# Weights four rows to a partition, X kept in the same order of columns: windowed attention with sinks and a highway layer on one core

## The chip, the cores and the metric

The kernel runs on one core of a Trainium2 chip. The metric is the time of one execution in microseconds (us) of device time; shorter is better. A core has five engines that matter here. TensorE (PE) multiplies matrices; its loads of weights are a row of their own (PEld). VectorE (DVE) and ScalarE (ACT) work element by element. GpSimd (POOL) does so too, and it also issues the loads that change the type on their way. SyncE (SP) issues other transfers. Sixteen DMA engines move the data between the chip's memory and the core's. The profile comes from one execution; the times come from several.

## What is computed

There are 4 batches of 8 heads, 768 positions and a head dimension of 64. Each query sees the 128 newest keys up to its own and the first 4 keys (the sinks). The heads of a position, side by side, are the 512 features of a token; a highway layer follows over the 3072 tokens.

```python
keep = is_sink | in_window            # in_window: 0 <= i - j < 128, is_sink: j < 4
a = softmax(where(keep, q @ k.T / 8, -1e9))
x = (a @ v)                           # (4, 8, 768, 64) -> (3072, 512)
H = maximum(x @ w_h, 0)
T = 1 / (1 + exp(-(x @ w_t + b_t)))
out = T * H + (1 - T) * x
```

All inputs and the output are float32. The kernel computes in float16 with sums in float32.

## The kernel before, in words

The work is cut into 24 tiles of 128 tokens, six to a batch. A loop over the steps n (lines 593 to 691) keeps three tiles in work: in step n the scores of tile n, the value products of tile n-1 and the highway layer of tile n-2. The order of the instructions on each engine is the order in which the program writes them (line 741 fixes it), so an instruction that waits holds up everything behind it on its engine.

**On PE, in a step:** the masks (line 308) and score products of tile n (line 333), the bias of the gate (line 371), the sinks' share (line 379) and the value products of tile n-1 (lines 432 and 435), the gate of tile n-2 (line 471, weight `wt`), half of its hidden layer (line 492, weight `wh`), four transpositions of X of tile n-1 (line 461), and the other half of the hidden layer. Tiles 0 to 3 are handled apart: their gates run in steps 2 to 5, their hidden layers in steps 4 to 6 (lines 611, 659, 664), because `wh` comes late.

**On ACT:** the exponential of a tile's scores (line 421), the tanh of the gate (line 479), and the copy of the transposed X out of PSUM (line 466).

**On DVE:** the normalization (lines 443 and 445) divides the value products by their sums and writes X of the tile; `diff` (line 505) computes max(h, 0) - X into `DD`; `gated` (line 510) multiplies it by the gate; and `transpose_qk` (line 133) turns Q and K, which come in with rows of tokens, in blocks of 32 by 32.

**On POOL:** `finish` (line 516) adds X to the gated difference and gives float32; `cast_v` (line 150) turns V to float16 from step 6 on; `sink_values` (lines 290 and 291); and all issues of Q, K and weight loads that change float32 to float16 (lines 117, 204, 208). These issues go round eight semaphores in turn, and each waits until the load eight places earlier has landed. The output goes out from SP.

X is a tile of 128 tokens by 512 features in their natural order. The weights lie with feature kc * 128 + p in partition p, part kc, and the transposition of X takes 128 neighbouring columns at a time, so that both sides of the products meet. The program's preamble (lines 180 to 208) issues the first loads in the order: Q and K of the first segment of batch 0, K of the second, `wt`, the bias row, Q and K of the third, `wh`. The first loads of batch 1 come in step 2 (lines 623 to 625), further ones by a table (lines 559 to 561), and the places of the transpositions by another (lines 547 to 556) and by the lines 636 to 651.

Of the kernel before, what the change touches and what calls it, by code (L numbers as in the profile page):

```python
# [10 lines left out]
FP16 = mybir.dt.float16  # L11
# [3 lines left out]
ALU = mybir.AluOpType  # L15
# [22 lines left out]
def kernel(  # L38
# [13 lines left out]
    P = 128  # L52
    pe, act, dve, pool, sp = nc.tensor, nc.scalar, nc.vector, nc.gpsimd, nc.sync

    B, H, S, D = q.shape
# [5 lines left out]
    NT, DM = out.shape  # L61
# [57 lines left out]
            in_=(q, k)[which][b, :, t0:t0 + nt, :].rearrange(  # L119
                "(hg g) (r m) d -> g r hg (m d)", g=G, m=nt // 32)[g])  # L120

    def load_rows(b, i, which):
        for g in range(G):
            load_part(b, i, g, which)

    def transpose_qk(b, i, which, hgs=slice(0, HG)):
# [22 lines left out]
    def cast_v(n, engine):  # L149
        engine.tensor_copy(out=v_of(n)[:, :, 0:D], in_=V32[n])  # L150
# [50 lines left out]
    load_sinks(0, range(2, G))  # L201
    make_identity(nc, ident)
    load_rows(0, 1, 1)
    pool.dma_start(out=wt, in_=moe_w_t.rearrange("(kc p) of -> p kc of", p=P))
    pool.dma_start(out=brow[0:P:32, :], in_=moe_b_t.unsqueeze(0).to_broadcast([G, DM]))
    load_rows(0, 2, 0)
    load_rows(0, 2, 1)
    pool.dma_start(out=wh, in_=moe_w_h.rearrange("(kc p) of -> p kc of", p=P))

    dve.memset(ebias, _EXP_BIAS)  # L210
    for g in range(1, G):
# [68 lines left out]
    def sink_keys(b, engine=pool):  # L280
        for hg in range(HG):
            engine.tensor_tensor(
                out=sk[:, b, hg, :, 1],
                in0=tr[b][:, 1, hg, 0:NSINK, :].rearrange("p s e -> p e s").unsqueeze(2)
                .to_broadcast([P, 2, G, NSINK]),
                in1=skmask.unsqueeze(1).unsqueeze(3)
                .to_broadcast([P, 2, G, NSINK]), op=ALU.mult)

    def sink_values(b):
        pool.tensor_copy(out=vs32[64:P, b, 0:D], in_=vs32[0:64, b, 0:D])  # L290
        pool.tensor_tensor(
            out=vs[b], in0=vs32[:, b].unsqueeze(1).to_broadcast([P, H, D + 1]),
            in1=vmask.unsqueeze(2).to_broadcast([P, H, D + 1]), op=ALU.mult)
# [146 lines left out]
    def norm(n):  # L440
        rec = work.tile([P, HG, G], FP32, tag="rec", name="rec")
        av = sums(n)[:, :, 0:G * (D + 1)].rearrange("p hg (g e) -> p hg g e", e=D + 1)
        dve.reciprocal(out=rec, in_=av[:, :, :, D])
        X[n] = work.tile([P, HG, G, D], FP16, tag="X", name="X", bufs=10)
        dve.tensor_tensor(out=X[n], in0=av[:, :, :, 0:D],  # L445
                          in1=rec.unsqueeze(3).to_broadcast([P, HG, G, D]), op=ALU.mult)

    XT = [None] * N

# [6 lines left out]

    def x_transpose(n):
        xt = turned(n)
        x = X[n].rearrange("p hg g d -> p (hg g d)")
        for kc in range(KC):  # L460
            pe.transpose(xt[:, kc // 2, (kc % 2) * P:(kc % 2 + 1) * P],  # L461
                         x[:, kc * P:(kc + 1) * P], ident)

    def x_copy(n):
        XT[n] = work.tile([P, KC * P], FP16, tag="XT", name="XT")
# [30 lines left out]

    O = [None] * N

    def flat(x, cols):
        return x.rearrange("p hg g d -> p (hg g d)")[:, cols]  # L500

    def diff(n, cols=slice(0, DM), h=None):
        if DD[n] is None:
            DD[n] = work.tile([P, DM], FP16, tag="DD", name="DD", bufs=8)
        dve.scalar_tensor_tensor(out=DD[n][:, cols], in0=ps_h[:, cols] if h is None else h,  # L505
                                 scalar=0.0, in1=flat(X[n], cols),
                                 op0=ALU.max, op1=ALU.subtract)

    def gated(n, cols=slice(0, DM)):
# [3 lines left out]
    def finish(n, cols=slice(0, DM), eng=pool, queue=sp):  # L513
        if O[n] is None:
            O[n] = work.tile([P, DM], FP32, tag="O", name="O")
        eng.tensor_tensor(out=O[n][:, cols], in0=DD[n][:, cols], in1=flat(X[n], cols),  # L516
                          op=ALU.add)
        queue.dma_start(out=out[n * P:(n + 1) * P, cols], in_=O[n][:, cols])

# [9 lines left out]
    def finish_twice(n, cols=slice(0, DM), queue=sp):  # L529
        if O[n] is None:  # L530
            O[n] = work.tile([P, DM], FP32, tag="O", name="O")
        dve.scalar_tensor_tensor(out=O[n][:, cols], in0=DD[n][:, cols], scalar=0.5,  # L532
                                 in1=flat(X[n], cols), op0=ALU.mult, op1=ALU.add)
        queue.dma_start(out=out[n * P:(n + 1) * P, cols], in_=O[n][:, cols])

    def complete(m):
# [20 lines left out]
    issues = [(b, i, g, which) for b in range(1, B) for i in range(len(segments[b]))  # L557
              for which in range(2) for g in range(G)][2 * G:]
    loads = {}
    for n, count in zip(range(2, 17), [4] * 4 + [3] * 7 + [2] + [3] * 3):  # L560
        loads[n] = [issues.pop(0) for _ in range(count)]
    assert not issues
    v_at = {1: (2,), 2: (3,), 3: (4,), 4: (5,), 5: (6, 7), 6: (8, 9)}
# [23 lines left out]
    transpose_qk(0, 1, 0)  # L587
    cast_v(0, dve)
    sink_keys(0, dve)

    idle(18)
    last = N - 1
    for n in range(last):

        nb, n1 = n - 2, n - 1
        joined = n < 5 or n >= 7
        before = (n1 if 0 <= n1 < N else None, nb if nb >= 0 else None)
        if n < N:
            after = opening(n, *before) if joined else scores(n)
            expo(n)  # L600
            if n in (4, 5):
                gate_value(n - 4)
            if n > NC and n % NC == NC - 1:
                gate_value(n - 3)
            for m in v_at.get(n, ()):
                if m < N:
                    load_v(m, after if n < 6 else None)
            if n % NC == 3 and n // NC + 1 < B:
                load_sinks(n // NC + 1)
        if 5 <= n <= 6:  # L610
            hidden(1 if n == 5 else 3)
        if n == 0:
            idle(5)
        if not joined:
            opening(None, *before)
        if 0 <= n1 < N:
            values(n1)
        if n >= 6:
            cast_v(n, pool)
        if NC <= n < N and n % NC == 0:  # L620
            sink_keys(n // NC)
        if n == 2:
            sink_values(0)
            load_rows(1, 0, 0)
            load_rows(1, 0, 1)
        for b, i, g, which in loads.get(n, ()):
            load_part(b, i, g, which)
        if n > NC and n % NC == 1:
            sink_values(n // NC)

        done = list(completed.get(n, ()))
        if n == 6:
            while done:
                complete(done.pop(0))
        turn = list(units.get(n, ()))
        if n == 5:
            transpose_qk(*turn.pop(0))
        if 5 <= n <= 6:
            diff(1 if n == 5 else 3)
        if 0 <= n1 < N:  # L640
            norm(n1)
        if n == 3:
            transpose_qk(0, 2, 1)
        if n == 2:
            transpose_qk(0, 2, 0)
        if n == 1:
            transpose_qk(0, 1, 1)
        if 0 < n < 4:
            cast_v(n, dve)
        for unit in turn:  # L650
            transpose_qk(*unit)
        if n == 5:
            cast_v(n, dve)

        if nb >= 0:
            gate(nb)
            tanh(nb)
        if n == 4:
            hidden(0)
            diff(0)  # L660
            cast_v(n, dve)
        if n == 5:
            gate_value(2)
            hidden(2)
        if n == 1:
            idle(3)
        if 6 <= n <= N:
            hidden(nb, range(KC // 2))
        if 0 <= n1 < N:
            x_transpose(n1)  # L670
            if n in sinks_at:
                sink_scores(*sinks_at[n])
            x_copy(n1)
            if n in sinks_at:
                sink_expo(*sinks_at[n])
            if nb >= N - 4:
                gate_value(nb)
        if 6 <= n <= N:
            hidden(nb, range(KC // 2, KC))
        if n in ahead:  # L680
            gate_value(ahead[n], pool)
        if n == last - 1:
            cast_v(last, pool)
        for m in done[:-1]:
            complete(m)
        if n == 5:
            diff(2)
        if 6 <= n <= N:
            diff(nb)
        for m in done[-1:] if n < last - 1 else ():  # L690
            complete(m)
# [32 lines left out]
    for part, cols, h, queue in ((0, left, h_left, sp), (1, right, ps_h[:, right], act)):  # L724
        gate(last, cols, gate_of(last, part))
        tanh(last, cols, gate_of(last, part))
        gate_value(last, cols=cols)
        hidden(last, cols=cols, into=h)
        if part == 1:

            for i, x in enumerate((flat(X[last - 1], slice(0, DM)), DD[last - 1])):
                pe.matmul(o_sum, lhsT=ident, rhs=x, start=(i == 0), stop=(i == 1),
                          skip_group_check=True)
            O[last - 1] = work.tile([P, DM], FP32, tag="O", name="O")
            act.copy(out=O[last - 1], in_=o_sum)
            sp.dma_start(out=out[(last - 1) * P:last * P, :], in_=O[last - 1])
        diff(last, cols, h)
        gated(last, cols)
        finish(last, cols, dve, queue)
# [35 lines left out]
```

## Time and profile before

| what | value |
|---|---|
| time, median of 3 runs | 108.14 us (107.81 to 108.58) |
| the profiled execution: its own time | 108.8 us |
| its span, first to last instruction | 106.8 us |
| instructions | 4671 |
| mean granted TensorE clock | 0.996 of full speed |
| moved by DMA | 20.81 MB, mean 195 GB/s |

The busy tenths of the 40 slices of the span:

```profile
PE   5997785988779999999999999999999999999930
PEld 2333452555325545655565556555655565465610
DVE  6998647555497879889988987899889979998960
ACT  3386687779648598798868997898689978986750
POOL 6899549918797999999999999999577829778000
DMA  3999999999999988789999998999995763252523
```

A slice is 2.67 us long and a 9 means 90% or more. Rows of the order of time, quoted below, begin with the start in us from the span's start and the duration in us; then come the engine, the line of the program, the operation, the written tile, `<-` and what is read, the shapes and the count. What stands in brackets at the end is the time that the engine sat idle before it, and what ended that. Rows of groups give, behind the bar, the total busy time, the mean of one in ns and the idle time before them. In the table by stretches each engine has its busy time, then come the granted clock, the DMA engines' mean share and the rate in GB/s.

### The profile page before, as it was taken

Reading aid. Unit: us, or ns where it says so; the run is one execution under the profiler, and the core shown is the slowest. Engines: PE = TensorE matmul, PEld = TensorE weight load, DVE = VectorE, ACT = ScalarE, POOL = GpSimd, SP = SyncE. Lnnn points to the kernel's source line nnn. Section 1 sums busy time; section 2 is a strip of 40 time slices with the busy share of each in tenths; the row PEclk is TensorE's granted clock in tenths of the full one; section 3 lists DMA queues with packets and bytes.
Section 4 is the critical chain, followed back from the end, with each engine's and each line's share of the span. In section 5 each row is a group of like instructions: output and inputs, shape, how many; then the busy total and the mean of one; then the engine's idle time right before and its main releaser. Section 6 shows DMA issues by size and latency. Waiting matters only on the chain. (4 is left out here: it accounts for less than half of the span.)

```text
span 106.8 us, 4671 instructions
## 1 busy us (share of the span) xinstructions
PE 95.6 (90%) x1960; PEld 53.0 (50%) x1960; DVE 85.6 (80%) x187; ACT 80.5 (75%) x105; POOL 83.6 (78%) x139
## 2 busy tenths in 40 slices
PE   5997785988779999999999999999999999999930
PEld 2333452555325545655565556555655565465610
DVE  6998647555497879889988987899889979998960
ACT  3386687779648598798868997898689978986750
POOL 6899549918797999999999999999577829778000
PEclk9999999999999999999999999999999999999998
DMA  3999999999999988789999998999995763252523
GB/s 77 225 260 225 200 215 196 151 179 232 212 213 237 176 151 240 133 213 250 223 208 269 250 249 190 235 235 211 221 296 126 201 181 114 104 198 84 214 84 114
DMA packets 36388, 20.81 MB, mean 195 GB/s; under 512 B 27020, under 2 KB 32912, under 8 KB 36368
## 3 DMA queue, kind: packets, MB, share of 16 engines
q1 hardware_dynamic: 29216, 13.31, 47.1%
q0 software_dynamic: 6848, 6.82, 40.7%
q10 hardware_dynamic: 304, 0.39, 1.2%
q8 instruction: 15, 0.25, 1.0%
q14 instruction: 5, 0.04, 0.1%
HBM read 21.05 MB, written 6.29 MB: 256 GB/s over the span
## 5 line engine op out<-in xcount | busy, mean ns | idle before, releaser
L421 ACT ACTIVATE E<-ps_s,ebias 128x2048 f16<-128x2048 f32 (+1 forms) x24 | 43.8, 1824 | 10.8 <-PE ps_s L333 10.8
L133 DVE STREAM_TRANSPOSE tr<-nat 128x384 f32<-128x384 f32 (+1 forms) x28 | 26.1, 962 | 3.7 <-DMA nat<-in_q_dram 2.1
L492 PE MATMUL ps_h<-wh,XT 128*128 128x512 f16 (+1 forms) x96 | 27.2, 375 | 1.8 <-DVE DD L505 1.8
L117 POOL DMA_DIRECT2D nat<-in_k_dram x40 | 21.8, 549 | 7.0 <-DMA wh<-in_moe_w_h_dram 2.6
L516 POOL TENSOR_TENSOR O<-DD,X 128x512 f32<-128x512 f16 x19 | 22.0, 1160 | 6.6 <-DVE DD L510 4.0
L471 PE MATMUL ps_z<-wt,XT 128*128 128x512 f16 (+1 forms) x96 | 24.3, 374 | 0.0
L505 DVE SCALAR_TENSOR_TENSOR DD<-ps_h,X 128x512 f16<-128x512 f32 (+1 forms) x24 | 16.1, 673 | 3.6 <-PE ps_h L492 3.6
L117 POOL DMA_DIRECT2D nat<-in_q_dram x32 | 17.8, 562 | 0.2
L466 ACT COPY XT<-ps_av 128x512 f16<-128x512 f16 x23 | 13.5, 586 | 4.4 <-PE ps_av L461 2.2
L445 DVE TENSOR_TENSOR X<-ps_av,rec 128x512 f16<-128x512 f32 x23 | 15.9, 691 | 0.8
L479 ACT ACTIVATE TH<-ps_z 128x512 f16<-128x512 f32 (+1 forms) x24 | 14.0, 582 | 3.2 <-PE ps_z L471 3.2
L333 PE MATMUL ps_s<-tr 32*64 32x192 f16 (+3 forms) x768 | 13.3, 240 | 1.2 <-DVE tr L133 1.2
L435 PE MATMUL ps_av<-v,E 128*128 128x65 f16 x184 | 13.4, 193 | 0.2
L492 PEld LDWEIGHTS <-XT 128*128 128x128 f16 x100 | 8.8, 98 | 8.4 <-issue 2.3
L432 PEld LDWEIGHTS <-E 128*128 128x128 f16 x160 | 10.3, 97 | 4.1 <-issue 3.2
L432 PE MATMUL ps_av<-v,E 128*128 128x65 f16 x152 | 12.4, 194 | 0.0
L435 PEld LDWEIGHTS <-E 128*128 128x128 f16 x192 | 11.8, 97 | 0.7 <-issue 0.6
L150 POOL CAST v<-V 128x512 f16<-128x512 f32 x18 | 11.9, 663 | 0.0
L333 PEld LDWEIGHTS <-tr 32*64 32x64 f16 x768 | 10.3, 104 | 1.9 <-issue 1.0
L471 PEld LDWEIGHTS <-XT 128*128 128x128 f16 x100 | 8.2, 98 | 5.9 <-issue 0.5
L510 DVE TENSOR_TENSOR DD<-DD,TH 128x512 f16<-128x512 f16 (+1 forms) x23 | 10.1, 444 | 0.8
L461 PEld LDWEIGHTS <-X 128*128 128x128 f16 x96 | 5.8, 97 | 9.5 <-DVE X L445 8.9
(90 smaller groups left out, 115.0 us busy)
## 6 DMA issues: line engine op xcount, KB each, us to landing
V<-in_v_dram SPq DMA_DIRECT2D x24, 256.0 KB, 4.7
out_dram<-O SPq DMA_DIRECT2D x23, 256.0 KB, 3.7
nat<-in_k_dram POOLq DMA_DIRECT2D x24, 64.0 KB, 4.6
nat<-in_q_dram POOLq DMA_DIRECT2D x16, 96.0 KB, 4.7
nat<-in_k_dram POOLq DMA_DIRECT2D x16, 96.0 KB, 4.6
nat<-in_q_dram POOLq DMA_DIRECT2D x16, 64.0 KB, 5.6
first<-in_q_dram SPq DMA_DIRECT2D x6, 128.0 KB, 3.7
wt<-in_moe_w_t_dram POOLq DMA_DIRECT2D x1, 512.0 KB, 7.3
```

Source lines behind the costliest of these rows:

```text
L117: engine.dma_start(out=into[32 * g:32 * g + 32].rearrange("p hg m d -> p hg (m d)"), in_=(q, k)[which][b, :, t0:t0 + nt, :].rearrange("(hg ...
L133: dve.transpose(out=dst, in_=src)
L333: return pe.matmul(ps_s[ks, g, hg, q0:q1], lhsT=tr[b][rows, 1, hg, k0:k0 + K2, e], rhs=tr[b][rows, 0, hg, c * P + q0:c * P + q1, e], start ...
L421: act.activation(out=E[n][:, :, :, 0:nq * P], in_=ps_s[:, :, :, 0:nq * P], func=AF.Exp, bias=ebias, scale=SCALE)
L432: pe.matmul(slot, lhsT=E[n - 1][:, g, hg, P:2 * P], rhs=v_of(n - 1)[:, h, :], start=first, stop=False, skip_group_check=True)
L435: pe.matmul(slot, lhsT=E[n][:, g, hg, 0:P], rhs=v_of(n)[:, h, :], start=first, stop=True, skip_group_check=True)
L445: dve.tensor_tensor(out=X[n], in0=av[:, :, :, 0:D], in1=rec.unsqueeze(3).to_broadcast([P, HG, G, D]), op=ALU.mult)
L471: pe.matmul(into, lhsT=XT[n][:, kc * P:(kc + 1) * P], rhs=wt[:, kc, cols], start=False, stop=(kc == KC - 1), skip_group_check=True)
L479: act.activation(out=TH[n][:, cols], in_=ps_z if z is None else z, func=AF.Tanh, scale=0.5)
L492: pe.matmul(into, lhsT=XT[n][:, kc * P:(kc + 1) * P], rhs=wh[:, kc, cols], start=(kc == 0), stop=(kc == KC - 1), skip_group_check=True)
L505: dve.scalar_tensor_tensor(out=DD[n][:, cols], in0=ps_h[:, cols] if h is None else h, scalar=0.0, in1=flat(X[n], cols), op0=ALU.max, op1=A ...
L516: eng.tensor_tensor(out=O[n][:, cols], in0=DD[n][:, cols], in1=flat(X[n], cols), op=ALU.add)
```

## The change

The weights are loaded with feature 4p + kc in partition p, part kc: each partition takes four neighbouring rows, which lie side by side in memory. For the products to meet, X is kept as four parts, part kc holding the features 4f + kc; so the normalization writes X in that order, with neighbouring features 128 elements (256 bytes) apart, the transposition takes one part at a time, and everything that adds or subtracts X in the natural order (lines 505, 516, 532, and the last product, line 732) reads it with that step, through the new function `natural`.

Besides, the order changes at the start. The bias row is loaded ahead of `wt`. `wh` leaves the preamble's block of loads; it now comes behind `sink_values(0)` and the first of the four Q loads of batch 1, still ahead of the loop. One load by the table moves from step 13 to step 17. Of the transpositions on DVE, that of K of the third segment of batch 0 is cut in two halves, one in step 2 and one in step 3; that of Q of batch 1 in step 4 moves behind the hidden layer's difference of tile 0; that of K in step 5 moves from before the difference of tile 1 to behind the normalization of tile 4.

```diff
-    pool.dma_start(out=wt, in_=moe_w_t.rearrange("(kc p) of -> p kc of", p=P))
     pool.dma_start(out=brow[0:P:32, :], in_=moe_b_t.unsqueeze(0).to_broadcast([G, DM]))
+    pool.dma_start(out=wt, in_=moe_w_t.rearrange("(p kc) of -> p kc of", kc=KC))
     load_rows(0, 2, 0)
     load_rows(0, 2, 1)
-    pool.dma_start(out=wh, in_=moe_w_h.rearrange("(kc p) of -> p kc of", p=P))
...
-        X[n] = work.tile([P, HG, G, D], FP16, tag="X", name="X", bufs=10)
-        dve.tensor_tensor(out=X[n], in0=av[:, :, :, 0:D],
-                          in1=rec.unsqueeze(3).to_broadcast([P, HG, G, D]), op=ALU.mult)
+        X[n] = work.tile([P, KC, P], FP16, tag="X", name="X", bufs=10)
+        dve.tensor_tensor(out=X[n].rearrange("p kc (hg g d) -> p hg g d kc", hg=HG, g=G),
+                          in0=av[:, :, :, 0:D].rearrange("p hg g (d kc) -> p hg g d kc", kc=KC),
+                          in1=rec.unsqueeze(3).unsqueeze(4).to_broadcast([P, HG, G, D // KC, KC]),
+                          op=ALU.mult)
...
-                         x[:, kc * P:(kc + 1) * P], ident)
+                         X[n][:, kc], ident)
...
-    def flat(x, cols):
-        return x.rearrange("p hg g d -> p (hg g d)")[:, cols]
+    def natural(x, cols=slice(0, DM)):
+        return x[:, :, cols.start // KC:cols.stop // KC].rearrange("p kc f -> p f kc")
...
-                                 scalar=0.0, in1=flat(X[n], cols),
+                                 scalar=0.0, in1=natural(X[n], cols),
...
-        eng.tensor_tensor(out=O[n][:, cols], in0=DD[n][:, cols], in1=flat(X[n], cols),
+        eng.tensor_tensor(out=O[n][:, cols], in0=DD[n][:, cols], in1=natural(X[n], cols),
...
-    for n, count in zip(range(2, 17), [4] * 4 + [3] * 7 + [2] + [3] * 3):
+    for n, count in zip(range(2, 18), [4] * 4 + [3] * 7 + [1] + [3] * 3 + [1]):
...
     sink_keys(0, dve)
+    sink_values(0)
+    load_rows(1, 0, 0, range(1))
+    pool.dma_start(out=wh, in_=moe_w_h.rearrange("(p kc) of -> p kc of", kc=KC))
...
         if n == 2:
-            sink_values(0)
-            load_rows(1, 0, 0)
+            load_rows(1, 0, 0, range(1, G))
             load_rows(1, 0, 1)
...
-        if n == 5:
-            transpose_qk(*turn.pop(0))
...
         if n == 3:
-            transpose_qk(0, 2, 1)
+            transpose_qk(0, 2, 1, slice(1, 2))
...
+        if n == 2:
+            transpose_qk(0, 2, 1, slice(0, 1))
+        for unit in turn if n != 4 else ():
             transpose_qk(*unit)
...
             diff(0)
+            transpose_qk(*turn.pop())
```

More of the change, by code (lines that the diff above doesn't have):

```diff
@@ L120, in load_part, with load_rows @@
                 "(hg g) (r m) d -> g r hg (m d)", g=G, m=nt // 32)[g])
-    def load_rows(b, i, which):
-        for g in range(G):
+    def load_rows(b, i, which, gs=range(G)):
+        for g in gs:
             load_part(b, i, g, which)
@@ L458, in x_transpose @@
         xt = turned(n)
-        x = X[n].rearrange("p hg g d -> p (hg g d)")
         for kc in range(KC):
             pe.transpose(xt[:, kc // 2, (kc % 2) * P:(kc % 2 + 1) * P],
-                         x[:, kc * P:(kc + 1) * P], ident)
+                         X[n][:, kc], ident)
     def x_copy(n):
@@ L532, in finish_twice @@
         dve.scalar_tensor_tensor(out=O[n][:, cols], in0=DD[n][:, cols], scalar=0.5,
-                                 in1=flat(X[n], cols), op0=ALU.mult, op1=ALU.add)
+                                 in1=natural(X[n], cols), op0=ALU.mult, op1=ALU.add)
         queue.dma_start(out=out[n * P:(n + 1) * P, cols], in_=O[n][:, cols])
@@ L649 @@
             cast_v(n, dve)
-        for unit in turn:
+        if n == 2:
+            transpose_qk(0, 2, 1, slice(0, 1))
+        for unit in turn if n != 4 else ():
             transpose_qk(*unit)
@@ L729 @@
         if part == 1:
-            for i, x in enumerate((flat(X[last - 1], slice(0, DM)), DD[last - 1])):
+            for i, x in enumerate((natural(X[last - 1]), DD[last - 1])):
                 pe.matmul(o_sum, lhsT=ident, rhs=x, start=(i == 0), stop=(i == 1),
```

## The prediction

> **What bounds the kernel now.** I read the page's busy shares and slices first, then a table by stretches, then the order of time on each engine. The first says that four engines are nearly full; the slices say where.
>
> ```profile
> PE 95.6 (90%) x1960; PEld 53.0 (50%) x1960; DVE 85.6 (80%) x187; ACT 80.5 (75%) x105; POOL 83.6 (78%) x139
> ```
> ```profile
> core 0: us, PE busy (x) PEld busy (x) DVE busy (x) ACT busy (x) POOL busy (x), PEclk, DMA share, GB/s
> 10.00:35.00 25.00, 19.79 (x462) 11.35 (x462) 15.63 (x30) 18.80 (x21) 18.19 (x33) 1.00 1.18 205
> 35.00:76.00 41.00, 40.75 (x924) 23.26 (x929) 36.52 (x70) 34.13 (x40) 40.61 (x65) 1.00 1.00 215
> 76.00:100.00 24.00, 23.89 (x508) 13.28 (x488) 22.03 (x42) 19.96 (x24) 16.27 (x20) 1.00 0.58 165
> 35.00:100.00 65.00, 64.64 (x1412) 36.54 (x1410) 58.56 (x111) 54.09 (x64) 56.88 (x84) 1.00 0.85 196
> ```
> There are three stretches. From 10 to 35 us no engine is full (PE idles 5.2 us) and the DMA engines are: the start waits for data. From 35 to 76 us PE and POOL are both full, POOL with 40.6 of 41 us. From 76 us POOL has 7.7 us to spare and PE alone is full. A busy PE by itself proves little, since ends of matmuls are modelled, so I asked who is on time for whom. Every tile needs its V cast (line 150, on POOL) before its value products (lines 432 and 435, on PE):
>
> ```profile
> 44.55 0.60 POOL L150 CAST v<-V 128x512 f16<-128x512 f32 x1
> 47.87 0.61 POOL L150 CAST v<-V 128x512 f16<-128x512 f32 x1
> 74.48 1.17 POOL L516 TENSOR_TENSOR O<-DD,X 128x512 f32<-128x512 f16 x1
> 75.59 0.62 POOL L150 CAST v<-V 128x512 f16<-128x512 f32 x1
> 77.30 1.15 POOL L516 TENSOR_TENSOR O<-DD,X 128x512 f32<-128x512 f16 x1 [1.09 <-issue]
> ```
> ```profile
> 44.95 0.20 PE L432 MATMUL ps_av<-v,E 128*128 128x65 f16 x1
> 45.21 0.19 PE L435 MATMUL ps_av<-v,E 128*128 128x65 f16 x1
> 48.51 0.20 PE L432 MATMUL ps_av<-v,E 128*128 128x65 f16 x1
> 76.58 0.20 PE L432 MATMUL ps_av<-v,E 128*128 128x65 f16 x1
> ```
> The cast that starts at 44.55 ends at 45.15, and PE, which had begun with the older tile's product at 44.95, goes on at 45.21. The next cast ends at 48.48 and PE begins at 48.51. So POOL hands PE its data at the last moment; by 76.21 against 76.58 there are 0.37 us in hand. POOL works without a gap from 35 to 76 us, so whatever lengthens its instructions there lengthens the kernel.
>
> **The edits to the start.** The waits there:
>
> ```profile
> 14.75 1.05 POOL L117 DMA_DIRECT2D nat<-in_k_dram  x2 [2.18 <-DMA wt<-in_moe_w_t_dram]
> 24.33 0.53 POOL L117 DMA_DIRECT2D nat<-in_k_dram  x1 [2.64 <-DMA wh<-in_moe_w_h_dram]
> 29.44 0.53 POOL L117 DMA_DIRECT2D nat<-in_k_dram  x1 [0.86 <-DMA nat<-in_k_dram]
> 34.53 0.53 POOL L117 DMA_DIRECT2D nat<-in_k_dram  x1 [0.70 <-DMA nat<-in_k_dram]
> ```
> ```profile
> 18.62 0.55 PE L333 MATMUL ps_s<-tr 32*64 32x192 f16 x32 [0.84 <-DVE tr L133]
> 22.09 0.55 PE L333 MATMUL ps_s<-tr 32*64 32x192 f16 x32 [0.37 <-DVE tr L133]
> 27.49 1.02 PE L492 MATMUL ps_h<-wh,XT 128*128 128x512 f16 x4 [1.08 <-DVE DD L505]
> 31.03 1.02 PE L492 MATMUL ps_h<-wh,XT 128*128 128x512 f16 x4 [0.72 <-DVE DD L505]
> ```
> ```profile
> 25.81 1.11 DVE L133 STREAM_TRANSPOSE tr<-nat 128x512 f32<-128x512 f32 x1 [1.32 <-DMA nat<-in_q_dram]
> 29.35 1.11 DVE L133 STREAM_TRANSPOSE tr<-nat 128x512 f32<-128x512 f32 x1 [1.40 <-DMA nat<-in_k_dram]
> ```
> POOL's loads go round eight semaphores: each issue waits for the landing of the load eight places earlier. That is why a late weight (wt, wh) stops an issue that has nothing to do with it, and why the last K load of the first segment of batch 1, issued only at 24.33, stops POOL twice more (0.86 and 0.70).
>
> *Load order.* In the new order the bias row goes before wt, and wh goes behind the first Q load of batch 1, with the sink values ahead of both. The order of instructions shows that it is now the first Q load of the next segment that waits for wh, and the K load issues before it. POOL gains that issue (0.53) and, if the loads land sooner, the two waits (1.56): 0.5 to 2.1 us. The lower end is real, because the DMA engines are full there (share 1.18). I take 1.5, nearest the two waits, since their cause, the late K issue, is removed. wt is issued behind one more load of POOL: its first use comes late enough that I count 0; if not, gate 0 waits some 0.5 us in a stretch where PE has idle time.
>
> *Weights as 128 rows of four.* The same bytes, in 128 long pieces in place of 512. A weight's issue takes 0.78 us and a 64-piece load 0.55, so up to 0.23 us less on POOL for each, twice; it lies in the waits and I count it as 0.
>
> *Transpositions moved.* On DVE the two that waited 1.32 and 1.40 us stood in front of a difference (line 505) for which PE waited (1.08, 0.72). They now stand behind the difference and behind the normalization. The halved one takes half of its 0.95 us from in front of the scores at 22.09 (0.37 there). That is 2.2 us of PE's waits. What is late next: the moved transposition of Q pushes the second difference by its own 0.95, of which PE sees perhaps 0.3, and the second half of K is only ready shortly before the scores of tile 6; the half transposition in step 2 also stands in front of a normalization and waits for the last K load. I put 0.7 back and take 1.5 us, bounds 0 and 2.2. So PE and POOL both enter the full stretch about 1.5 us earlier; these leads are the same time, not a sum.
>
> **X kept in the order of the weights' rows.** X is now written by line 445 with four neighbouring columns 256 bytes apart, and read by lines 505 (DVE), 516 (POOL), 532 and 732 with that step. The counts do not change; the question is what a step of 256 bytes costs.
>
> ```profile
> L516 POOL TENSOR_TENSOR O<-DD,X 128x512 f32<-128x512 f16 x19 | 22.0, 1160 | 6.6 <-DVE DD L510 4.0 <-issue 2.5
> L117 POOL DMA_DIRECT2D nat<-in_k_dram x40 | 21.8, 549 | 7.0 <-DMA wh<-in_moe_w_h_dram 2.6 <-DMA wt<-in_moe_w_t_dram 2.2 <-DMA nat<-in_k_dram 1.8
> L150 POOL CAST v<-V 128x512 f16<-128x512 f32 x18 | 11.9, 663 | 0.0
> L505 DVE SCALAR_TENSOR_TENSOR DD<-ps_h,X 128x512 f16<-128x512 f32 (+1 forms) x24 | 16.1, 673 | 3.6 <-PE ps_h L492 3.6
> ```
> ```profile
> 12.38 0.69 DVE L445 TENSOR_TENSOR X<-ps_av,rec 128x512 f16<-128x512 f32 x1
> 12.98 1.10 DVE L133 STREAM_TRANSPOSE tr<-nat 128x512 f32<-128x512 f32 x1
> 13.93 0.41 DVE L150 CAST v<-V 128x512 f16<-128x512 f32 x1
> ```
> No row has this step on POOL. The nearest row with a wide step is the transposition, whose writes are 8 floats apart: 0.95 us from its start to the next one's, where the X instruction with the same 512 elements takes 0.60. That is 0.35 us per 512 elements, if all of it is the step. On POOL the lower bound is 0 and the upper one a second input that costs twice what it does: two-input 1160 less one-input 663 is about 0.5. Between them I take 0.35. A period of POOL is three load issues, a cast and a finish: 3 x 0.55 + 0.66 + 1.16 = 3.5 us, and becomes 3.8.
>
> On POOL a rule of the Trainium skill speaks against the change: GPSIMD Engine Reference, section 7, says that reads with a step over 8 bytes take about 2.9 cycles per element where others take 1.9. At the page's 1.2 GHz that is an estimate of 0.43 us per finish; the sum below would be 3.3 us longer by it instead of 2.3. No run shown so far can test it.
>
> On DVE I take 0, with bounds 0 and 0.35: X's instruction takes 1.17 ns per element already, where the cast in the row behind the transposition takes 0.41 us in all for the same 512, so it has no fast rate that it could lose; not below 0, since nothing is left out. The one strided matmul pair of line 732 lies in the tail and costs at most its own length again, 0.4 us each, beside DVE work that ends later; 0.
>
> *The sum.* Twelve finishes stand in POOL's queue between 37 us and the cast at 75.59:
>
> ```profile
> 37.68 2.28 POOL L516 TENSOR_TENSOR O<-DD,X 128x512 f32<-128x512 f16 x2
> ```
> is the first two and the one at 74.48 the last. 12 x 0.35 = 4.2 us, less the lead of 1.5 and the 0.37 in hand, leaves 2.3 us at the value products of tile 17. Behind that POOL's spare 7.7 us cover the other seven finishes. The profiled execution took 108.8 us (span 106.8 and 2.0 around it), which is 0.7 above the median of 108.14. Its sum is 111.1; from the median it is 110.4. I forecast 110.8.
>
> **The rivals.**
>
> *Steps are free everywhere.* Then only the start counts: 1.5 us less, 106.6 from the median. For it: the 1.17 ns per element that X costs already; against it, the transposition's 0.95 us. It decides from a finish that stays under about 1.16 + 0.13 us, where 12 times the excess is smaller than the lead. Chance 0.27.
>
> *DVE pays too.* X's instruction and the difference each take 0.35 more, 0.70 per tile. From 35 to 100 us DVE has 65 - 58.56 = 6.4 us free and would need 18 x 0.70 = 12.6 more, so it runs over by 6.2 and becomes the bound; less the lead, 4.7, and about one more for the idle time that it can't fill: 114. For it: X is handed over at the last moment too:
>
> ```profile
> 49.52 0.69 DVE L445 TENSOR_TENSOR X<-ps_av,rec 128x512 f16<-128x512 f32 x1
> 50.30 0.39 PE L461 MATMUL ps_av<-ident,X 128*128 128x128 f16 x4
> ```
> It ends at 50.21 and PE turns it at 50.30, so every delay of X beyond 0.09 reaches PE. Chance 0.28. The Trainium skill has a rule behind this one: SBUF — State Buffer, section "Door 1", speaks of 16-byte lines of which each should be hit twice. It gives no price; the transposition's 0.95 us against 0.60 agrees with a price for writes of at most 0.35.
>
> *The start gains nothing and steps cost little.* The DMA engines are full, so the loads land when they did, and a finish costs 0.1 more: within 1% of 108. Chance 0.08.
>
> **How the numbers follow.** The forecast, POOL's finish alone, has 0.37, with its own range 109 to 113 (0.2 to 0.5 per finish and a lead of 0.5 to 2.1). One per cent, 1.08 us, is about what a measurement of this kernel can tell from no change. Faster by more holds with free steps, 0.27; within it are the last rival and the forecast's cheapest corner, 0.10; slower are the rest of the forecast and the DVE case, 0.63. The range reaches from the free case, 106.3, to above the DVE case, 116.
>
> **What would show it.** In the profile after: the mean of the finish on POOL (1160 before; 1.5 us expected), of X (691) and of the difference (673; unchanged expected). The waits of PE for the difference at 27 and 31 us should be gone. The casts should stay just ahead of the value products from 40 to 76 us, with longer periods. I am wrong if the finish stays at 1.16, if X or the difference rises, or if PE's first full stretch begins no earlier than 35 us.

## The result, and the profile after

The changed kernel takes 155.8 us in the median of six runs (153.96 to 157.87), the kernel before 108.19. The ratio is 1.430, with a 95% interval from 1.423 to 1.437. Single executions of one kernel lie up to 4% apart, so the ratios, here and below, compare only those within 1.5% of each kernel's fastest, while the medians are of all. The forecast was 110.8 us with a range up to 116. The direction was right, the size was not: 47.6 us came, 2.6 were forecast.

The profiled execution took 156.67 us, with a span of 154.7 where 106.8 had been. The page's busy shares of the changed kernel:

```profile
PE 106.5 (69%) x1960; PEld 56.7 (37%) x1960; DVE 132.8 (86%) x188; ACT 82.3 (53%) x105; POOL 87.4 (56%) x139
```

DVE's busy time rose from 85.6 to 132.8 us, POOL's from 83.6 only to 87.4. The added work is nearly all on one engine. The groups of instructions of X, of the finish and of the difference, each with busy time and mean in ns behind the first bar, say where. The first row is X before; the others are of the changed kernel and have its line numbers (446 was 445, 463 was 461, 494 was 492, 508 was 505, 513 was 510, 519 was 516):

```profile
L445 DVE TENSOR_TENSOR X<-ps_av,rec 128x512 f16<-128x512 f32 x23 | 15.9, 691 | 0.8
L446 DVE TENSOR_TENSOR X<-ps_av,rec 128x512 f16<-128x512 f32 x23 | 56.0, 2433 | 0.8
L519 POOL TENSOR_TENSOR O<-DD,X 128x512 f32<-128x512 f16 x19 | 27.2, 1435 | 46.1 <-DVE DD L513 34.3 <-issue 8.5 <-DMA V<-in_v_dram 3.3
L508 DVE SCALAR_TENSOR_TENSOR DD<-ps_h,X 128x512 f16<-128x512 f32 (+1 forms) x24 | 24.5, 1021 | 6.0 <-PE ps_h L494 6.0
```

The write of X in four parts takes 2433 ns where 691 had been. The difference takes 1021 where 673 had been, the finish on POOL 1435 where 1160 had been. The finish is 0.27 us longer, near the 0.35 that the forecast had taken. But POOL now idles 46.1 us in front of it, mostly for DVE, and no wait of PE or DVE for a product of POOL is left among the profile's waits. The waits of the changed kernel (total, times, longest) show who is late:

```profile
PEld L463 <- DVE X L446: 51.4, 24, 2.6
PE ps_av L463 <- DVE X L446: 37.7, 23, 2.1
POOL O L519 <- DVE DD L513: 34.3, 13, 5.4
```

One tile in the order of time on DVE, in the middle of the span:

```profile
70.30 0.20 DVE L444 RECIPROCAL rec<-ps_av 128x8 f32<-128x8 f32 x1
70.54 2.43 DVE L446 TENSOR_TENSOR X<-ps_av,rec 128x512 f16<-128x512 f32 x1
72.59 1.04 DVE L133 STREAM_TRANSPOSE tr<-nat 128x384 f32<-128x384 f32 x1
74.56 1.05 DVE L508 SCALAR_TENSOR_TENSOR DD<-ps_h,X 128x512 f16<-128x512 f32 x1 [0.93 <-PE ps_h L494]
75.52 0.29 DVE L488 TENSOR_SCALAR TH<-TH 128x512 f16<-128x512 f16 x1
75.85 0.43 DVE L513 TENSOR_TENSOR DD<-DD,TH 128x512 f16<-128x512 f16 x1
77.05 0.21 DVE L444 RECIPROCAL rec<-ps_av 128x8 f32<-128x8 f32 x1 [0.77 <-PE ps_av L436]
```

and the same place on PE:

```profile
70.40 0.59 PE L494 MATMUL ps_h<-wh,XT 128*128 128x512 f16 x2
73.03 0.58 PE L463 MATMUL ps_av<-ident,X 128*128 128x128 f16 x4 [2.03 <-DVE X L446]
```

From one reciprocal to the next is 6.75 us in this step. PE stands 2.03 us before the transposition of X, because X is finished only at 72.97. Behind that wait the hidden layer is late, so DVE in turn waits 0.93 us for it, and then 0.77 for the next value products. This step is longer than most, since the granted clock of TensorE was 0.50 to 0.55 from 73 to 76 us: the transposition takes 0.58 us here where it took 0.39 before. Over the 17 steps from the reciprocal at 42.15 us to that at 138.38 the mean is 5.66 us. Before the change it was 3.54 (16 steps, from 38.27 to 94.92). The 2.1 us between them are about what X (1.74) and the difference (0.35) are longer.

### The profile page after: what moved, and what is told of

It reads as the page before. It is cut to its first block, busy times and chain, and to the rows that moved or that the text cites. A ratio compares the mean times of both kernels' runs of the same rounds, so it can differ in the third digit from the quotient of the medians.

```text
span 154.7 us, 4672 instructions
## 1 busy us (share of the span) xinstructions
PE 106.5 (69%) x1960; PEld 56.7 (37%) x1960; DVE 132.8 (86%) x188; ACT 82.3 (53%) x105; POOL 87.4 (56%) x139
## 5 line engine op out<-in xcount | busy, mean ns | idle before, releaser
L446 DVE TENSOR_TENSOR X<-ps_av,rec 128x512 f16<-128x512 f32 x23 | 56.0, 2433 | 0.8
L519 POOL TENSOR_TENSOR O<-DD,X 128x512 f32<-128x512 f16 x19 | 27.2, 1435 | 46.1 <-DVE DD L513 34.3
L463 PE MATMUL ps_av<-ident,X 128*128 128x128 f16 x92 | 9.5, 229 | 37.7 <-DVE X L446 37.7
L133 DVE STREAM_TRANSPOSE tr<-nat 128x384 f32<-128x384 f32 (+2 forms) x29 | 30.1, 1063 | 0.6 <-DMA nat<-in_k_dram 0.4
L508 DVE SCALAR_TENSOR_TENSOR DD<-ps_h,X 128x512 f16<-128x512 f32 (+1 forms) x24 | 24.5, 1021 | 6.0 <-PE ps_h L494 6.0
L334 PE MATMUL ps_s<-tr 32*64 32x192 f16 (+3 forms) x768 | 15.2, 265 | 1.2 <-DVE tr L133 1.2
L436 PE MATMUL ps_av<-v,E 128*128 128x65 f16 x184 | 15.5, 205 | 0.0
L433 PE MATMUL ps_av<-v,E 128*128 128x65 f16 x152 | 13.8, 207 | 0.0
L436 PEld LDWEIGHTS <-E 128*128 128x128 f16 x192 | 13.5, 105 | 0.7 <-issue 0.6
L433 PEld LDWEIGHTS <-E 128*128 128x128 f16 x160 | 11.9, 105 | 4.6 <-issue 4.1
L444 DVE RECIPROCAL rec<-ps_av 128x8 f32<-128x8 f32 x23 | 4.7, 202 | 8.7 <-PE ps_av L436 8.7
L494 PEld LDWEIGHTS <-XT 128*128 128x128 f16 x100 | 9.0, 100 | 7.6 <-issue 1.8
```

Source lines behind the costliest of these rows:

```text
L133: dve.transpose(out=dst, in_=src)
L334: return pe.matmul(ps_s[ks, g, hg, q0:q1], lhsT=tr[b][rows, 1, hg, k0:k0 + K2, e], rhs=tr[b][rows, 0, hg, c * P + q0:c * P + q1, e], start ...
L433: pe.matmul(slot, lhsT=E[n - 1][:, g, hg, P:2 * P], rhs=v_of(n - 1)[:, h, :], start=first, stop=False, skip_group_check=True)
L436: pe.matmul(slot, lhsT=E[n][:, g, hg, 0:P], rhs=v_of(n)[:, h, :], start=first, stop=True, skip_group_check=True)
L446: dve.tensor_tensor(out=X[n].rearrange("p kc (hg g d) -> p hg g d kc", hg=HG, g=G), in0=av[:, :, :, 0:D].rearrange("p hg g (d kc) -> p hg ...
L494: pe.matmul(into, lhsT=XT[n][:, kc * P:(kc + 1) * P], rhs=wh[:, kc, cols], start=(kc == 0), stop=(kc == KC - 1), skip_group_check=True)
```

## The experiments

Ten kernels ran. Ratios are to the kernel before, run beside it on the same chip, with their 95% intervals.

**1. What a step costs, one instruction at a time.** Single instructions of 512 elements follow the kernel's last output, three of each. Their data mean nothing.

```diff
+    for _ in range(3): dve.tensor_tensor(out=w16(1), in0=z, in1=ones_in, op=ALU.mult)
+    for _ in range(3): dve.tensor_tensor(out=w16(2), in0=z, in1=ones_in, op=ALU.mult)
+    for _ in range(3): dve.tensor_tensor(out=w16(4), in0=z, in1=ones_in, op=ALU.mult)
+    for _ in range(3): dve.tensor_tensor(out=w16(8), in0=z, in1=ones_in, op=ALU.mult)
...
+    for _ in range(3): dve.tensor_tensor(out=parts(sc, 136).rearrange('p (a f) kc -> p a f kc', a=8), in0=zz, in1=in4, op=ALU.mult)
...
+    for _ in range(3): pe.matmul(ps_h, lhsT=ident, rhs=r16(8), start=True, stop=True, skip_group_check=True)
```

> The kernel before with single instructions behind its last output, each three times: the writes of X's instruction and the reads of the difference, of the finish, of ACT and of TensorE, with 512 elements and other steps. Three theories of why X's instruction went from 0.69 to 2.43 us. Line theory: what counts is that neighbouring elements lie 16 or more bytes apart, whatever the distance. Then writes with steps of 2, 4 and 8 bytes take 0.69 us, steps of 16 and 24 bytes and the four parts take 2.4, at a pitch of 256 as of 272 bytes, and a 4-byte write with a step of 16 bytes is slow too. Bank theory: the power of two counts. Then the four parts take 2.4 us at 256 bytes and about 0.7 at 272 or 260. Narrow-write theory: a lone 2-byte write costs a read and a write of what surrounds it. Then the write with a step of 4 bytes already takes 2.4 us, and 4-byte writes in four parts of 512 bytes take at most 1.1. Reads: 1.04 us in four parts on DVE and 1.43 on POOL are known; by the line theory the rise comes between 8 and 16 bytes, by the bank theory not at 272.

The groups of this kernel, for writes on DVE. Lines 768 to 772 write float16 with steps of 2, 4, 8, 16 and 24 bytes; 773 to 775 float32 with steps of 4, 8 and 16 bytes; 776 and 777 float16 in four parts 256 and 272 bytes apart; 779 float32 in four parts 512 bytes apart:

```profile
L768 DVE TENSOR_TENSOR tr<-ps_z,rec 128x512 f16<-128x512 f32 x3 | 2.1, 692 | 0.1
L769 DVE TENSOR_TENSOR tr<-ps_z,rec 128x512 f16<-128x512 f32 x3 | 2.2, 732 | 0.1
L770 DVE TENSOR_TENSOR tr<-ps_z,rec 128x512 f16<-128x512 f32 x3 | 3.9, 1307 | 0.1
L771 DVE TENSOR_TENSOR tr<-ps_z,rec 128x512 f16<-128x512 f32 x3 | 7.4, 2462 | 0.1
L772 DVE TENSOR_TENSOR tr<-ps_z,rec 128x512 f16<-128x512 f32 x3 | 7.2, 2399 | 0.1
L773 DVE TENSOR_TENSOR tr<-ps_z,rec 128x512 f32<-128x512 f32 x3 | 2.3, 756 | 0.1
L774 DVE TENSOR_TENSOR tr<-ps_z,rec 128x512 f32<-128x512 f32 x3 | 2.1, 691 | 0.1
L775 DVE TENSOR_TENSOR tr<-ps_z,rec 128x512 f32<-128x512 f32 x3 | 3.2, 1053 | 0.1
L776 DVE TENSOR_TENSOR tr<-ps_z,rec 128x512 f16<-128x512 f32 x3 | 7.3, 2431 | 0.1
L777 DVE TENSOR_TENSOR tr<-ps_z,rec 128x512 f16<-128x512 f32 x3 | 7.1, 2352 | 0.1
L779 DVE TENSOR_TENSOR tr<-ps_z,rec 128x512 f32<-128x512 f32 x3 | 3.3, 1095 | 0.1
```

Reads of float16 beside contiguous writes, on DVE with steps of 8 and 16 bytes and in parts of 256 bytes (783, 784, 786); a read of PSUM with a step of 16 bytes (788); reads on POOL with steps of 8 and 16 bytes and in parts (793, 794, 796); and a write in parts on POOL (798) and on ACT (800):

```profile
L783 DVE SCALAR_TENSOR_TENSOR tr<-ps_z,tr 128x512 f16<-128x512 f32 x3 | 2.1, 691 | 0.1
L784 DVE SCALAR_TENSOR_TENSOR tr<-ps_z,tr 128x512 f16<-128x512 f32 x3 | 3.1, 1047 | 0.1
L786 DVE SCALAR_TENSOR_TENSOR tr<-ps_z,tr 128x512 f16<-128x512 f32 x3 | 3.0, 1014 | 0.1
L788 DVE CAST tr<-ps_z 128x512 f16<-128x512 f32 x3 | 2.1, 691 | 0.1
L793 POOL TENSOR_TENSOR tr<-tr,tr 128x512 f32<-128x512 f16 x3 | 3.5, 1159 | 0.2
L794 POOL TENSOR_TENSOR tr<-tr,tr 128x512 f32<-128x512 f16 x3 | 4.1, 1382 | 0.2
L796 POOL TENSOR_TENSOR tr<-tr,tr 128x512 f32<-128x512 f16 x3 | 4.3, 1427 | 0.2
L798 POOL TENSOR_TENSOR tr<-tr 128x512 f16<-128x512 f16 x3 | 7.4, 2462 | 0.2
L800 ACT ACTIVATE tr<-ps_z 128x512 f16<-128x512 f32 x3 | 7.3, 2442 | 34.8 <-POOL tr L798 34.8
```

These rows decide between the three theories. The bank theory falls: 272 bytes (2352 ns) are as bad as 256 (2431). Neither of the other two stands alone. The line theory had 8 bytes free for writes; they take 1307. The narrow-write theory had 4 bytes at 2.4 us; they take 0.73. Its other half, four-byte elements in four parts at 1.1 us at most, holds (1095). What fits is both together. On DVE, reads of two-byte elements cost nothing extra at 8 bytes (691 ns) and half as much again at 16 (1047), and no more in four parts (1014). Writes of two-byte elements nearly double from 4 to 8 bytes and again from 8 to 16 and then stay. That would fit a price for every move of such a write to another stretch of 16 bytes: 256 moves at a step of 8 bytes, 512 at 16, at 24 and in four parts. No step between 8 and 16 bytes was run, so this reading isn't shown. Four-byte elements at 16 bytes take 1053 ns where two-byte ones take 2462. Why a lone two-byte write costs more than a four-byte one, no run shows. A rival does fall: while line 776 ran, from 134.6 us of this execution, no other engine worked and nothing moved, and the write took the 2431 ns that it takes in the kernel (2433). So the price is no contention between engines.

**2. The order alone.** Weights and X go back to the layout of before; the load order and the moved transpositions stay.

```diff
+        X[n] = work.tile([P, HG, G, D], FP16, tag="X", name="X", bufs=10)
+        dve.tensor_tensor(out=X[n], in0=av[:, :, :, 0:D],
+                          in1=rec.unsqueeze(3).to_broadcast([P, HG, G, D]), op=ALU.mult)
...
+    pool.dma_start(out=wt, in_=moe_w_t.rearrange("(kc p) of -> p kc of", p=P))
```

> The changed kernel with weights and X in the layout of before; only the load order and the moved transpositions are left. Theory (the whole loss is the step of X): 106.6 us from 108.2, a gain of 0.5 to 2.2, X at 691 ns and the finish at 1160. Rival (the start gains nothing, since the DMA engines are full): within 0.4 us of 108.2. A second rival (the order is part of the loss): 109 or more.

Measured: ratio 1.002 (0.997 to 1.007). The order gains nothing and loses nothing that can be told, as the first rival had it. PE's two waits for the difference (1.08 and 0.72 us before) are down to one of 0.19. But POOL, in the order of time of this kernel, is not earlier:

```profile
16.10 0.54 POOL L117 DMA_DIRECT2D nat<-in_k_dram  x1 [3.27 <-DMA wt<-in_moe_w_t_dram]
25.33 2.13 POOL L117 DMA_DIRECT2D nat<-in_q_dram  x4 [2.25 <-DMA wh<-in_moe_w_h_dram]
35.50 0.62 POOL L150 CAST v<-V 128x512 f16<-128x512 f32 x1
```

```profile
41.00 0.19 PE L436 MATMUL ps_av<-v,E 128*128 128x65 f16 x1 [0.53 <-POOL v L150]
```

```profile
10.00:35.00 25.00, 20.83 (x465) 12.04 (x465) 17.07 (x34) 18.89 (x21) 17.61 (x33) 1.00 1.12 196
35.00:76.00 41.00, 39.52 (x889) 22.56 (x886) 36.25 (x68) 33.90 (x39) 40.48 (x64) 1.00 1.01 215
```

The first V cast starts at 35.50 us (35.06 before). The gate of tile 4 starts on PE at 34.01 (34.75 before), and seven microseconds later PE gives 0.53 of that back, waiting for a cast. In the table by stretches PE has done 1.0 us more work by 35 us than before (20.83 against 19.79), and 1.2 less between 35 and 76 us (39.52 against 40.75), where POOL is full. In this execution, which took 109.21 us, the lead existed on one engine only.

**3. X natural, turned with a step.** The weights keep four rows to a partition. X is written and read side by side; only the transpositions on TensorE take every fourth column.

```diff
-            pe.transpose(xt[:, kc // 2, (kc % 2) * P:(kc % 2 + 1) * P],
-                         X[n][:, kc], ident)
+        x = X[n].rearrange("p hg g d -> p (hg g d)").rearrange("p (f kc) -> p kc f", kc=KC)
...
+            pe.transpose(xt[:, kc // 2, (kc % 2) * P:(kc % 2 + 1) * P],
+                         x[:, kc], ident)
```

> The changed kernel with X back in the natural order, written and read side by side; the weights stay four rows to a partition, and the four transpositions on TensorE take every fourth column, a step of 8 bytes in the loads of X as weights. Theory (only steps on DVE and POOL cost): 106.6 us, the same as with the order alone or 0.3 less for the larger pieces of the weights. Rival (TensorE pays for a step of 8 bytes too): the loads of X rise from 97 ns to 200 or more, 0.4 us per tile on PE, 115 us.

Measured: 107.38 us, ratio 0.992 (0.988 to 0.995). The whole loss is gone, and a little more. The rival's 200 ns for a load of X do not come. The loads do get longer, from 97 to 115 ns in the mean; over 96 loads that is 1.7 us, and it does not show in the time.

**4. The write contiguous, the reads in parts.**

```diff
+        for hg in range(HG):
+            dve.tensor_tensor(out=X[n].rearrange("p kc (hg g d) -> p hg kc g d", hg=HG, g=G)[:, hg],
+                              in0=av[:, hg, :, 0:D].rearrange("p g (d kc) -> p kc g d", kc=KC),
+                              in1=rec[:, hg].unsqueeze(1).unsqueeze(3).to_broadcast([P, KC, G, D // KC]),
+                              op=ALU.mult)
```

> The changed kernel, but X's instruction is cut in two (one for each half of the heads) and goes part by part: it writes 16 neighbours side by side and reads PSUM with a step of 16 bytes. The reads of X in four parts by the difference and the finish stay. Theory (the step of the write is what costs): each half takes 0.4 to 0.5 us, X 0.2 to 0.3 longer than before per tile; with the difference at 1.04 and the finish at 1.43, 112 to 118 us. Rival (a step in PSUM costs as much as one in SBUF): each half takes 1.2 us and the kernel stays at 150 to 155.

Measured: 117.6 us, ratio 1.089 (1.083 to 1.094). The group of X in this kernel:

```profile
L447 DVE TENSOR_TENSOR X<-ps_av,rec 128x256 f16<-128x256 f32 x46 | 17.4, 420 | 0.8
```

The same X in the same place, filled in another order of its elements, costs two times 420 ns instead of 2433. Some 37 us of the loss hang on which neighbour is written next. Reading PSUM with a step of 16 bytes costs nothing: line 788 of experiment 1 takes 691 ns, and so does the same copy with a contiguous read (line 789).

**5 to 7. One step at a time.** In experiment 5 X is written and turned as in the changed kernel, and read side by side; in 6 only the difference, in 7 only the finish reads in parts, on the kernel of experiment 3. The columns that meet are the wrong ones in all three. The first cut is of experiment 5, the second of 6 and 7, where `apart` stands in for `natural` in the one instruction.

```diff
     def natural(x, cols=slice(0, DM)):
-        return x[:, :, cols.start // KC:cols.stop // KC].rearrange("p kc f -> p f kc")
+        return x.rearrange("p kc f -> p (kc f)")[:, cols]
```

```diff
+    def apart(x, cols=slice(0, DM)):
+        return x.rearrange("p hg g d -> p (hg g d)").rearrange("p (kc f) -> p f kc", kc=KC)[
+            :, cols.start // KC:cols.stop // KC]
...
```

> The changed kernel in which X is still written in four parts and turned so, but the difference, the finish and the last product read it side by side, in the wrong order of columns: the output's values are not the reference's. Only the write's step costs. Theory (the write is nearly the whole loss, and it lies on the path of every tile): X at 2.43 us, difference 0.68, finish 1.16; 24 x 1.74 = 42 us more than the natural X, 146 to 150 us. Rival (the three steps feed each other, and DVE would have time for the write alone): 135 or less.

Measured: 147.66 us, ratio 1.367 (1.360 to 1.373). The groups of X, and of the finish, in this kernel:

```profile
L446 DVE TENSOR_TENSOR X<-ps_av,rec 128x512 f16<-128x512 f32 x23 | 56.0, 2435 | 0.8
L519 POOL TENSOR_TENSOR O<-DD,X 128x512 f32<-128x512 f16 x19 | 21.9, 1154 | 42.7 <-DVE DD L513 33.6 <-issue 7.4 <-DMA V<-in_v_dram 1.7
```

The write alone, with the reads at their old price, makes some 40 of the 47 us between experiment 3 and the changed kernel, by the ratios; 24 x 1.74 = 42 had been expected. The rest is left for the two reads. The difference alone would make 24 x 0.35 = 8, and POOL waits for DVE. How much of it the lower granted clock made (0.924 in the changed kernel's profile, 0.964 in this one) is not shown.

> The kernel with natural X and strided turning (107.4 us), in which the difference alone reads X in four parts, so it subtracts the wrong columns. The difference takes 1.04 instead of 0.68 us, 0.36 per tile. Theory (DVE has some 6 us free between 35 and 100 us and takes in most of 18 x 0.36 = 6.5): 108 to 111 us. Rival (every length on DVE reaches PE, because X is handed over at the last moment): 24 x 0.36 = 8.6 more, 116 us.

Measured: 112.99 us, ratio 1.035 (1.028 to 1.042), between the two expectations. Of the 24 x 0.35 = 8 us some 5 came; DVE's free time would account for the others. PE waits 4.0 us for X, in ten places, where it waited 1.5 in four in experiment 3.

> The kernel with natural X and strided turning (107.4 us), in which only the finish reads X in four parts, so it adds the wrong columns; on POOL it takes 1.43 instead of 1.16 us. This is the recorded forecast's mechanism alone. Theory (POOL paces the middle stretch): 12 x 0.27 = 3.2 us, less at most 1.2 that POOL has in hand by then: 109.5 to 110.6. Rival (another engine paces it and POOL's 0.27 is hidden): 107.4 within 0.4.

Measured: 112.55 us, ratio 1.038 (1.031 to 1.045). The waits of PE for the casts are 1.4 us in two places in experiment 3, and here

```profile
PE ps_av L436 <- POOL v L150: 3.5, 6, 1.2
```

POOL paces the middle, as the forecast said. The cost is larger than the count, though: 12 x 0.29 = 3.5 us from this kernel's mean, and some 5 measured against experiment 3.

```profile
L522 POOL TENSOR_TENSOR O<-DD,X 128x512 f32<-128x512 f16 x19 | 27.6, 1459 | 5.1 <-DVE DD L516 3.7 <-issue 1.3
```

The rest is not explained.

**8. The weights alone**, in the order of before, with X natural and turned with a step of 8 bytes.

```diff
-    pool.dma_start(out=wt, in_=moe_w_t.rearrange("(kc p) of -> p kc of", p=P))
+    pool.dma_start(out=wt, in_=moe_w_t.rearrange("(p kc) of -> p kc of", kc=KC))
...
-    pool.dma_start(out=wh, in_=moe_w_h.rearrange("(kc p) of -> p kc of", p=P))
+    pool.dma_start(out=wh, in_=moe_w_h.rearrange("(p kc) of -> p kc of", kc=KC))
```

> The kernel before in its own order, with the weights four rows to a partition and X natural, turned with a step of 8 bytes. Theory (the larger pieces alone give the 0.8% of the kernel with natural X and strided turning, by 0.2 us less issue on POOL for each weight and an earlier landing): 107.2 to 107.6. Rival (only together with the new order, which gives PE its lead while the pieces give POOL its own): 108.0 to 108.4.

Measured: 107.12 us, ratio 0.988 (0.983 to 0.992). Like experiment 3 this is faster than the kernel before, by about 1%; four of its six executions took 106.17 to 107.18 us, the other two 108.92 and 109.23. Two more pairs, on other chips, differ in the same edit alone: experiments 3 and 2 (0.992 and 1.002) and, below, 10 and 9 (1.000 and 1.009). Each time the weights four rows to a partition, with X turned in steps, are about 1% shorter. The issue of wt on POOL takes 584 ns where 782 had been (the kernel before above):

```profile
L204 POOL DMA_DIRECT2D wt<-in_moe_w_t_dram x1 | 0.8, 782 | 0.0
L204 POOL DMA_DIRECT2D wt<-in_moe_w_t_dram x1 | 0.6, 584 | 0.0
```

The profiled execution took 108.92 us, as long as the kernel before, so where the gain arises is not shown.

**9 and 10. wt ahead of the bias row again.** Experiment 2 suggested that the later wt holds POOL back. Number 9 is experiment 2 and number 10 experiment 3 with these two issues exchanged.

```diff
-    pool.dma_start(out=brow[0:P:32, :], in_=moe_b_t.unsqueeze(0).to_broadcast([G, DM]))
     pool.dma_start(out=wt, in_=moe_w_t.rearrange("(kc p) of -> p kc of", p=P))
+    pool.dma_start(out=brow[0:P:32, :], in_=moe_b_t.unsqueeze(0).to_broadcast([G, DM]))
```

> The kernel with the new order and all layouts of before, but wt is issued ahead of the bias row again. With the order alone, wt was issued 0.6 us later, POOL stood 3.27 us before a K load that waits for wt, and its first V cast came at 35.50 us, not earlier than the 35.06 of the kernel before, so PE's lead of 0.7 us was lost waiting for a later cast. Theory (that later wt is what keeps the order from gaining): the wait for wt falls to about 2.2, the casts come some 1 us earlier, and the time is 107.2 to 107.6. Rival (the DMA engines are full, so POOL's lead does not come whatever waits first): 108.0 to 108.5, the casts at 35 us and later.

> The same issue order with the weights four rows to a partition and natural X turned with a step of 8 bytes: every part of the change that can gain, without a step on DVE or POOL. Theory (POOL's lead from the order and from the pieces add): 106.4 to 107.0. Rival (POOL's lead is limited by the data, once is all): 107.0 to 107.5, like the weights alone.

Measured: ratios 1.009 (1.004 to 1.013) and 1.000 (0.995 to 1.005), medians 109.07 and 108.53 us. Both theories fall, and both times lie above the rival's too: they are 0.7 to 0.8% longer than experiments 2 and 3, whose order differs only in these two issues, though those ran on another chip. In number 9, POOL's wait for wt does fall to 2.04 us, but POOL then waits longer for wh, and PE waits for wh as well:

```profile
25.59 2.10 POOL L117 DMA_DIRECT2D nat<-in_q_dram  x4 [2.98 <-DMA wh<-in_moe_w_h_dram]
35.19 0.63 POOL L150 CAST v<-V 128x512 f16<-128x512 f32 x1
```

```profile
25.35 1.02 PE L493 MATMUL ps_h<-wh,XT 128*128 128x512 f16 x4 [1.30 <-DMA wh<-in_moe_w_h_dram]
```

Here something else of the same data lands late, and the first cast stays at 35 us (35.09 in number 10). That is the rival's reading, and what the forecast's third rival said of the start. But 35 us is no fixed limit: in the profile of experiment 3 the first cast started at 33.93 us. Which load's landing sets it, and what makes numbers 9 and 10 longer, stays open.

## Why the prediction was wrong

**The step that failed** is "On DVE I take 0, with bounds 0 and 0.35". X's instruction rose by 1.74 us, five times the upper bound. The difference rose by 0.35, just at it. The bound came from the transposition's writes, which also jump. But those write four-byte elements, and X has two-byte ones. Experiment 1 has four-byte elements 16 bytes apart at 1053 ns, 0.36 us more than at 8 bytes, just as the bound had it, and two-byte ones at 2462. The nearest row shared a wide step and not the size of the element. I had asked only how far the step was. The other argument, that X's instruction has no fast rate to lose, was no bound either: the same instruction went from 691 to 2433 ns.

**The choice between the forecast and its rival** followed from that. "DVE pays too" named the right place: X is handed over 0.09 us before PE needs it, so a longer X delays every tile. Its price, 0.35 for each of the two instructions, gave 114 us. With 1.74 for X, the path through X gives 24 x 1.74 = 42 us, and experiment 5 measured 40.

**The finish on POOL** was right in itself: 0.27 us longer where 0.35 was taken. Alone it does what the forecast said, in direction: experiment 7 stands at 112.55 us, inside the forecast's own range. In the changed kernel no cost of it shows, since POOL waits for DVE. So the right direction is luck as far as that kernel goes: the finish, from which the forecast took it, is not what made it slower. The rule of the Trainium skill that the forecast set beside this step (GPSIMD Engine Reference, section 7) holds in its threshold: 8 bytes 1159 ns, 16 bytes 1382. The estimate from its figures, 0.43 us, was too high by half.

**The 16-byte lines** of the Trainium skill (SBUF — State Buffer, section "Door 1"), of which each should be hit twice, fit DVE's reads: 691 ns at 8 bytes, which is two elements to a line, 1047 at 16, and no more at 256. They do not fit the writes of two-byte elements: two to a line take 1307 ns instead of 692. The larger price was the one for writes, and one run of single instructions was needed to see it.

**The start.** Two statements held: PE's waits for the difference went, and with the order alone PE began its first full stretch 0.7 us earlier. The lead of 1.5 us did not reach the time (ratio 1.002), and POOL's part of it did not come at all: the first cast was 0.44 us later than before, which lies even below the lower bound of 0.5 us gained. I had taken 1.5 as "nearest the two waits"; their cause was removed, and in experiment 2 POOL stood longer for wt (3.27 us against 2.18) instead.

**Weights as 128 rows**, counted as 0, are worth about 1% by experiment 8 and the two other pairs. That term was mis-sized in the other direction. The 0.2 us of issue per weight that the forecast named is there; it was said to lie in the waits. How it becomes 1 us of the time stays open.

## What to carry to other kernels

Before a layout is turned, ask of every instruction that writes or reads it how far apart its neighbours lie, and how wide they are: a layout that one load or one matmul likes is paid for by all the others. Where a permutation is needed, let the loop go along the destination and put the step on the side that reads, as experiment 4 does from PSUM, or into TensorE's loads of weights at 8 bytes, as experiments 3 and 8 do. And where full engines hand over at the last moment, a bound taken from an unlike row is not a bound: measure the single instruction first; it takes one run.

## What the runs showed of the hardware that was not expected

- The write of 512 two-byte elements in four parts takes about the same on three engines: 2431 ns on DVE, 2462 on POOL, 2442 on ACT, although the contiguous one takes 692 on DVE and 597 on ACT. Three engines with one price point to the memory rather than to an engine; no run shows it directly.
- TensorE's moving operand (the one that is not loaded as weights) pays as well, and from a smaller step than DVE's reads: 377 ns at 2 bytes, 386 at 4, 622 at 8, 1078 at 16 and 1043 in four parts (experiment 1). The granted clock was 1.00 for the first four and 0.50 for the four parts. Its loads of weights with a step of 8 bytes pay little: 115 ns against 97 in experiments 3 and 8.
- The granted clock of TensorE was 0.924 in the changed kernel's profile, against 0.996 before. Of its six executions the fastest (153.96 us) had 0.940 and the one with the lowest clock (0.904) took 157.65. No run tells what the clock cost.
